# An attention decode block with gradients: the step order and weight layout of the Wo product, and the width of the V times do sums

## The chip, the cores and the metric

One core of one Trainium2 chip. The metric is the device time of one execution in microseconds (us). The core has a matrix engine (PE, with PEld for its weight loads), a vector engine (DVE), a scalar engine (ACT), GpSimd (POOL), and SP, which here only issues DMAs. Sixteen DMA engines move data between the chip's memory (DRAM) and the core's on-chip memory. PE writes its results to PSUM, in banks that each hold 512 float32 values on each of 128 partitions.

## The reference, cut to what matters

One token goes through a block of attention and MLP whose layer norms are modulated by a condition c. The kernel computes the output and the gradients of nine inputs.

```python
def _A_ref(x, k_cache, v_cache, wq, wo):          # 32 heads, 8192 keys, 192 wide
    q = (x @ wq).reshape(B, Sq, Hq, Dh).transpose(0, 2, 1, 3)
    scores = einsum('bhqd,bhkd->bhqk', q, k_cache) * Dh ** (-0.5)
    p = softmax(scores, axis=-1)
    o = einsum('bhqk,bhkd->bhqd', p, v_cache)
    return o.transpose(0, 2, 1, 3).reshape(B, Sq, Hq * Dh) @ wo

sa, ca, ga, sb, cb, gb = (silu(c) @ w_mod) in six parts of 640
h = layernorm(x) * (1 + ca) + sa
x = x + ga * _A_ref(h, ...)
h = layernorm(x) * (1 + cb) + sb
x = x + gb * _B_ref(h, ...)       # h + gelu(layernorm(h) @ w3) @ w4
_out, _vjp = jax.vjp(_f, x, k_cache, v_cache, wq, wo, w3, w4, c, w_mod)
return (_out, *_vjp(grad_out))
```

All arrays are bf16. x is 1 x 640, wq 640 x 6144, wo 6144 x 640, w_mod 640 x 3840, and each of k_cache and v_cache is 32 heads x 8192 x 192, 100 MB. The gradients of the two caches are as large again and are written out whole. (A first layer of `_B_ref` shifts the one token out of the sequence and adds zeros; it is left away here.)

## The kernel before, in words

**Tiles.** A head's K or V is 8192 rows of 192. It is moved in two halves of 1536 KB, each with 32 neighbouring rows on each of 128 partitions, so a partition receives 12288 neighbouring bytes. There are five such tiles for K (`big`), three for V in the forward (`fv`), and three more from the backward on (`bv`); K's tiles later hold the outputs dK and dV.

**Queues and order.** SP issues, in program order, every load of K, V and Wo in the forward, every load of V in the backward and every store of dK and dV. An issue that waits for its tile holds up those behind it. POOL issues Wo's loads for the backward and the stores of the gradients of Wo and w4. The order on PE, DVE and ACT is the order of the program: `pin_order` (L53) ties each instruction to the one before it on its engine, from the first forward product on.

**Forward, L592 to L659.** A loop over heads, with three heads in work at a time: in iteration i the scores of head i are made, and the scaled keys and values of head i-1 are summed. For the scores, `fwd_mult` multiplies a half of K by q on DVE (tile `prod`), `fwd_ssum` (L372) sums 192 columns down to 8 with 48 matmuls against an identity, `fwd_red` (L376) sums the last 8 on DVE; then come the maximum and the exponent. For head i-1, ACT (L407) and DVE (L414) scale K by the exponents, a quarter head at a time (tile `EK`), and PE multiplies V with the scaled K: `fwd_kvA` (L432), `fwd_kvB` (L443), and `fwd_kvK` (L449) for the sum of K. The result is a 192 x 192 matrix for a head, kept for the backward, and in one more column the unscaled output o.

Pairs of heads share 384 rows of Wo. `fwd_wo` (L460) loads them once per pair, 480 KB, as three blocks of 128 rows: row 128 c + p goes to partition p. `fwd_o` (L481, in odd iterations) divides o by the sum of the exponents and leaves it in three columns of `o_col_bf`, in that order of rows. In the next, even iteration `fwd_ao` (L520) multiplies the three blocks with the three columns in 15 matmuls of one column, into columns 408 to 412 of a PSUM tile `sm_ps`, and `fwd_ao_add` adds them to `ao_c` on DVE. Then `fwd_tot` (L476) sums the exponents of the two newer heads over the partitions, into columns 400 and 401 of the same `sm_ps`, and `fwd_rinv` (L479) inverts them on DVE. `sm_ps` has one buffer of one bank. The calls stand so in the loop:

```python
        if i % 2 == 0 and i >= 4:
            fwd_ao((i - 4) // 2, st[i - 3]["wo"], st[i - 1]["sm"])
            fwd_ao_add((i - 4) // 2, st[i - 1]["sm"])
        if p and i % 2 == 0:
            fwd_tot(i - 1, st[i - 1]["sm"])
```

On DVE a half's `fwd_mult` stands ahead of `fwd_ao_add`. The last two pairs have their Wo kept for the backward, which reads it in blocks of 128 rows.

**Middle, L660 to L889 and on.** The rest of the block: layer norms, the MLP and its gradient, down to the gradient of the attention output.

**Backward, L1249 to L1317.** A loop over heads from the last to the first. `bwd_mult` (L1017) multiplies a half of V in place by do, the gradient of that head's output, broadcast to all partitions (L132, tile `V_sb`); 24 matmuls a half (L1025), each with 256 columns (32 rows times 8), sum 192 products to 8 in the PSUM tile `dP_ps`. `bwd_ds` (L1051) sums the 8 on DVE, 512 numbers on each partition, and makes dS. `bwd_dk` (L1008, tile `dK`) makes the two halves of dK as dS times q on DVE and stores them. `bwd_dv` makes the next head's dV as probability times do, 20 of 32 rows on ACT (L1030) and 12 on DVE (L1008, tile `dV`), and stores it. V comes through a ring of six tiles. `hook` (the first ten heads, NPH = 10) makes do for the later pairs from Wo; in those ten heads other steps of the PSUM pool `psum_b` need banks too. Later jobs (J0 to J2) make the gradients of wq and w_mod, their sums at L1137 in the tile `js_ps`.

Of the kernel before, what the change touches and what calls it, by code (L numbers as in the profile page):

```python
# [9 lines left out]
BF16 = mybir.dt.bfloat16  # L10
# [10 lines left out]
def kernel(  # L21
# [26 lines left out]
    nc = tc.nc  # L48
# [16 lines left out]
    P = 128  # L65
# [5 lines left out]
    J = S // P  # L71
# [9 lines left out]
    DS = 8  # L81
# [15 lines left out]
    def bank_s(name):  # L97
        return bank("s", 2, name)
# [98 lines left out]
    def dve_copy(out, in_):  # L197
        nc.vector.tensor_copy(out=out, in_=in_)
# [120 lines left out]
    ao_c = ccol(NDC, "ao_c")  # L319
    fsm_cm = tc.tile_pool(name="fsmall", bufs=2, reuse_waits="tile")  # L320
    fsm = fsm_cm.__enter__()

    def head_split(h):
        if h % 2 == 0:
# [8 lines left out]
    def load_fwd(h, t, kind):  # L333
        if not 0 <= h < HQ:
            return
        if kind == "v":
            st[h]["V"].append(load_v(fv, h, t, (2 * h + t) % 3))
        elif (h, t) not in K_st:
            K_st[h, t] = load_k(h, t)
# [116 lines left out]
    def fwd_wo(h, st):  # L456
        if h % 2 == 1:
            c0 = 3 * (h // 2)
            st["wo"] = fwo.tile([P, 3, D], BF16, name="wo_t")
            nc.sync.dma_start(out=st["wo"], in_=wo_v[:, c0 : c0 + 3, :])  # L460

    def fwd_keep(h, st):
        (a0, a1), (b0, b1), bp, ca_, cb_ = head_split(h)
# [11 lines left out]
    def fwd_tot(h, sm):  # L475
        nc.tensor.matmul(sm[:, 400:402], lhsT=ones_mat_f, rhs=rowsum[:, h - 1 : h + 1], start=True, stop=True)  # L476
# [4 lines left out]
    def fwd_o(hp):  # L481
        c0 = 3 * hp
        for h in (2 * hp, 2 * hp + 1):
            _, _, bp, ca_, cb_ = head_split(h)
            mul(o_col_f[:, ca_ : ca_ + 1], MA_all[:, h, DH : DH + 1], rinv_bc[:, h : h + 1])
            mul(o_col_f[bp : bp + 64, cb_ : cb_ + 1], MB_all[bp : bp + 64, hp, DH : DH + 1], rinv_bc[bp : bp + 64, h : h + 1])
        dve_copy(o_col_bf[:, c0 : c0 + 3], o_col_f[:, c0 : c0 + 3])
# [20 lines left out]
    def fwd_o_last(h, st):  # L508
        _, _, bp, ca_, cb_ = head_split(h)
        c0 = 3 * (h // 2)  # L510
        sl = slice(bp, bp + 64)
        mul(o_col_f[:, ca_ : ca_ + 1], st["o_ps"][:, 0:1], rinv_bc[:, h : h + 1])
        mul(o_col_f[sl, cb_ : cb_ + 1], st["o_ps"][sl, 1:2], rinv_bc[sl, h : h + 1])
        dve_copy(o_col_bf[:, c0 : c0 + 3], o_col_f[:, c0 : c0 + 3])

    def fwd_ao(hp, wo, sm, c1=408):
        c0 = 3 * hp
# [74 lines left out]
    for i in range(1, HQ):  # L592
        c, p, pp = 2 <= i < HQ, 0 <= i - 1 < HQ, 0 <= i - 2 < HQ
        n = i + 1 < HQ
        if p:
            fwd_scale(i - 1, 0, st[i - 1])
        if pp:
            fwd_kvA(i - 2, 3, st[i - 2])
            fwd_kvB(i - 2, 3, st[i - 2])
            fwd_kvK(i - 2, 3, st[i - 2])  # L600
            fwd_keep(i - 2, st[i - 2])
            fwd_keepB(i - 2, st[i - 2])
            if i % 2 == 1:
                fwd_o((i - 2) // 2)
        load_fwd(i, 0, "v")
        if p:
            fwd_wo(i - 1, st[i - 1])
        if c:
            fwd_ssum(i, 0, st[i])
        if p:  # L610
            fwd_scale(i - 1, 1, st[i - 1])
            fwd_kv(i - 1, 0, st[i - 1])
        load_fwd(i + 1, 1, "k")
        if c:
            fwd_mult(i, 1, st[i])
        if i % 2 == 0 and i >= 4:
            fwd_ao((i - 4) // 2, st[i - 3]["wo"], st[i - 1]["sm"])
            fwd_ao_add((i - 4) // 2, st[i - 1]["sm"])
        if p and i % 2 == 0:
            fwd_tot(i - 1, st[i - 1]["sm"])  # L620
        if i % 2 == 1 and n:
            q_pb[(i + 1) // 2] = pair_bc(fsm, q_bf, (i + 1) // 2, "q_pb", st[max(i - 1, 1)]["sm"])
        if p:
            fwd_scale(i - 1, 2, st[i - 1])
            if i % 2 == 0:
                fwd_rinv(i - 1, st[i - 1]["sm"])
            fwd_kv(i - 1, 1, st[i - 1])
        load_fwd(i, 1, "v")
        if c:
            fwd_ssum(i, 1, st[i])  # L630
        if p:
            fwd_scale(i - 1, 3, st[i - 1])
            if i == 1:
                q_out(1, NWQ)
        if c:
            fwd_red(i, st[i])
        if p:
            fwd_kvA(i - 1, 2, st[i - 1])
        if c:
            fwd_comb(i, st[i])  # L640
        if p:
            fwd_kvK(i - 1, 2, st[i - 1])
        if c:
            fwd_max(i, st[i])
        if p:
            fwd_kvB(i - 1, 2, st[i - 1])
        if c:
            fwd_exp(i, st[i])
        load_fwd(i + 2, 0, "k")
        if i == HQ - 2:  # L650
            load_w(0)
        if i == HQ - 1:
            fwd_wo(i, st[i])
            load_w(1)
            load_w(2)
        if n:
            fwd_mult(i + 1, 0, st[i + 1])
        if n:
            fwd_pairs(i, st[i])  # L659
# [356 lines left out]

    def bwd_mult(h, t, parts=1):  # L1017
        if t == 0:
            bst[h]["dP_ps"] = bank_s("dP_ps").rearrange("p (j d) -> p j d", d=DS)
        n = JH // parts  # L1020
        for r in range(0, JH, n):
            V_sb = V_b[h][t][:, r : r + n, :]
            mul(V_sb, V_sb, vec_of(do_pb, h)[:, None, :].to_broadcast([P, n, DH]))
            for k in range(NDS):
                nc.tensor.matmul(bst[h]["dP_ps"][:, t * JH + r : t * JH + r + n, :], lhsT=ident_bf, rhs=V_sb[:, :, k * DS : (k + 1) * DS], start=(k == 0), stop=(k == NDS - 1))  # L1025
        freed.add(("v", h, t))

    def bwd_dv_act(o, h, t, lo=0, hi=NAV // 2):
# [206 lines left out]
    pairs_outer(o1[:, 26:JH, :], bst[HS[1]]["P2h"][:, 26:JH, :], vec_of(do_pb, HS[1]), JH - 26)  # L1235
    bwd_dv_store(o1, HS[1], 0, JQ, JH)
    psum_cm.__exit__(None, None, None)
    psum[0] = ctx.enter_context(tc.tile_pool(name="psum_b", bufs=1, space=bass.MemoryType.PSUM, reuse_waits="tile"))
    CB[0], SB[0] = 2, 512
    tw_cm.__exit__(None, None, None)  # L1240
    bso = ctx.enter_context(tc.tile_pool(name="bso", bufs=2, reuse_waits="tile"))
# [7 lines left out]
    for i in range(HQ):  # L1249
        h, nxt = HS[i], HS[i + 1] if i + 1 < HQ else None  # L1250
        if i % 2 == 1 and i > NPH and nxt is not None:
            bwd_dob(nxt // 2)
        for f in J0[i]:
            f()
        if i <= AHEAD:
            if i in SPLIT:
                bwd_pf(nxt)
            for t in range(2):
                bwd_mult(h, t, 2 if i == 0 else 1)
                if i == t == 0:  # L1260
                    ring_load()
                    c_first = fin_c(PS[0], 1)
                if i in SPLIT:
                    bwd_dv(nxt, t)
        if i not in EARLY:
            ring_load()
        if i - 1 in dq:
            fin_dq(*dq.pop(i - 1))
        if i == 0:
            fin_c_copy(PS[0], 1, c_first)  # L1270
        if nxt is not None and i not in SPLIT:
            if i > 0:
                bwd_pf(nxt)
            for t in range(0 if i > 0 else 1, 2):
                bwd_dv(nxt, t)
        if i in EARLY:
            ring_load()
        if i == 0:
            bwd_ds(h)
            dq_last(h)  # L1280
        if i < NPH:
            hook(i)
        if i == 3:
            bcast_cols(du_bf, 0, NFC, du_bc, act_copy)
        for f in J1[i]:
            f()
        if i > 0:
            bwd_ds(h)
        if i >= AHEAD and nxt is not None:
            for t in range(2):  # L1290
                bwd_mult(nxt, t)
        bwd_dk(h, 0)
        bwd_dk(h, 1)
        if i in cps:
            fin_c_copy(*cps.pop(i))
        if i == 1:
            mid_cols()
            job_mid()
            dve_copy(dmod_bf[:, 2 * NDC : 6 * NDC], dmod_c[:, 2 * NDC : 6 * NDC])
        if i == NPH - 1:  # L1300
            fin_dq(*dq.pop(i))
            mm_cm.__exit__(None, None, None)
            for nm, b in (("out", 2), ("bcp", 1)):
                side_cm.append(tc.tile_pool(name="side" + nm, bufs=b, side="right", reuse_waits="tile"))
                side[nm] = side_cm[-1].__enter__()
        for f in J2[i]:
            f()
        if i == I_SIDE:
            while side_cm:
                side_cm.pop().__exit__(None, None, None)  # L1310
            xt = ctx.enter_context(tc.tile_pool(name="xt", bufs=1, side="right", reuse_waits="tile"))
            for k in "xyz":
                tail_tiles[k] = (xt, "xt" + k)
            for n in range(len(ring) - NR, len(ring)):
                slot = ring_slot(n)
                tail_tiles[f"v{n - len(ring) + NR}"] = (bv if slot > 2 else fv, f"v{slot}")
            big_order[:] = tail_list(big_order[0:5] + ["x", "y", "z"])  # L1317
# [31 lines left out]
```

## Time and profile before

| what | value |
| --- | --- |
| time, median of 3 runs | 1374.94 us (1373.59 to 1375.22) |
| the profiled execution | 1375.21 us |
| its span, first to last instruction | 1373.4 us |
| mean granted TensorE clock in it | 0.785 |
| busy: PE, DVE, ACT, POOL | 881.4, 1062.8, 916.5, 21.5 us |
| moved by DMA | 569.26 MB in 65006 packets, 414 GB/s on average |
| forward | until about 534 us of the span |
| backward loop, with its last stores | from about 590 us to the end |

The profile is one execution. Engine rows give busy time and its share of the span, with instructions behind the x. In rows of groups, `out<-in` names the tiles that are written and read; behind the bar stand busy time, the mean of one instruction in ns, the idle time of the engine just before such instructions, and what ended most of it. Rows of a timeline start with the time of the first instruction and the length of the group, and have in brackets the idle time before it. The slices cut the span into 40 equal parts and show each engine's busy tenths. "DMA share" is the share of the 16 DMA engines' time in which a packet is under way.

### The profile page before, as it was taken

To read this page: it belongs to the slowest core of one execution; us is meant where nothing else is said; L and a number is where in the kernel's file an instruction comes from. 1 tells how busy PE (TensorE), PEld (TensorE's weight loads), DVE (VectorE), ACT (ScalarE), POOL (GpSimd) and SP (SyncE) were. 2 spreads that over 40 slices of the span, in tenths; PEclk is the share of its full clock that TensorE was granted. 3 is DMA by queue.
4 is the path that set the end of the run, shared out by engine and by line. 5 is a ranking of instruction groups with operands and counts; after the bars stand their busy time and mean duration, and the time that the engine had idled before them with its cause. 6 is when DMAs were issued, how large, how long until landed. Compare 5 with 4: busy or idle time off the path is not lost.

```text
span 1373.4 us, 28399 instructions
## 1 busy us (share of the span) xinstructions
PE 881.4 (64%) x11743; PEld 686.0 (50%) x11743; DVE 1062.8 (77%) x1196; ACT 916.5 (67%) x2564; POOL 21.5 (2%) x33
## 2 busy tenths in 40 slices
PE   3699999999999999757756664534334344224430
PEld 3577777777777777746645552322223223113330
DVE  3488878878878877899977877966768778669990
ACT  1388877877877876886766768645577564547960
POOL 0000000000000000000000000000000000000000
PEclk9799999999999999576676676666656757656665
DMA  9999999999999999899999999999999999999997
GB/s 392 412 413 420 420 419 419 419 412 414 418 409 421 419 407 387 336 394 424 423 419 426 424 424 427 422 428 425 428 425 424 427 427 428 426 428 427 428 429 309
DMA packets 65006, 569.26 MB, mean 414 GB/s; under 512 B 6444, under 2 KB 14124, under 8 KB 23404
## 3 DMA queue, kind: packets, MB, share of 16 engines
q1 hardware_dynamic: 61182, 550.73, 96.1%
q0 software_dynamic: 3664, 16.71, 3.0%
q8 instruction: 92, 1.51, 0.4%
q14 instruction: 38, 0.31, 0.1%
q10 hardware_dynamic: 30, 0.00, 0.0%
HBM read 341.51 MB, written 225.91 MB: 413 GB/s over the span
## 4 chain that ended last, share of the span: by engine, by line
DMA 38%; DVE 28%; PE 23%; ACT 4%; SPq 2%; issue 2%; DVEq 0%; ACTq 0%
DMA out_dram<-dV 25%; DVE prod L132 9%; PE ps_a L432 8%; DVE dK L1008 6%; DMA out_dram<-dK 6%; DVE V_sb L132 6%; PE S_ps L372 4%; DMA V_sb<-in_A_v_cache_dram 3%; PE dP_ps L1025 3%; PE ps_b L443 3%; PE kb_ps L449 2%; DVE dV L1008 2%; DMA K_sb<-in_A_k_cache_dram 2%; ACT dV L1030 2%; ACT EK L407 2%
## 5 line engine op out<-in xcount | busy, mean ns | idle before, releaser
L1030 ACT ACTIVATE dV<-do_pb,PF 128x192 bf16<-128x192 bf16 x1246 | 436.0, 440 | 173.3 <-DMA out_dram<-dV 132.2
L1025 PE MATMUL dP_ps<-V_sb,ident_bf 128*128 128x256 bf16 (+1 forms) x1584 | 237.0, 326 | 203.8 <-DVE V_sb L132 203.5
L407 ACT ACTIVATE EK<-K_sb,E_f 128x192 bf16<-128x192 bf16 x992 | 351.1, 442 | 4.0 <-PE kb_ps L302 2.6
L1025 PEld LDWEIGHTS <-ident_bf 128*128 128x128 bf16 x1584 | 182.2, 119 | 260.9 <-DVE V_sb L132 170.7
L1008 DVE TENSOR_TENSOR dK<-dS,q_pb 128x6144 bf16<-128x6144 bf16 x64 | 212.6, 3354 | 15.7 <-DMA out_dram<-dK 12.0
L132 DVE TENSOR_TENSOR prod<-K_sb,q_pb 128x6144 bf16<-128x6144 bf16 x64 | 214.3, 3349 | 3.0 <-DMA K_sb<-in_A_k_cache_dram 3.0
L132 DVE TENSOR_TENSOR V_sb<-V_sb,do_pb 128x6144 bf16<-128x6144 bf16 (+1 forms) x66 | 212.3, 3253 | 0.0
L432 PE MATMUL ps_a<-EK,V_sb 128*128 128x193 bf16 x1984 | 195.7, 252 | 3.2 <-DMA V_sb<-in_A_v_cache_dram 3.2
L432 PEld LDWEIGHTS <-V_sb 128*128 128x128 bf16 x1984 | 168.3, 100 | 21.1 <-issue 12.5
L1008 DVE TENSOR_TENSOR dV<-P2h,do_pb 128x2304 bf16<-128x2304 bf16 (+2 forms) x67 | 89.8, 1353 | 113.9 <-DMA out_dram<-dV 111.8
L414 DVE TENSOR_TENSOR EK<-K_sb,P2h 128x1536 bf16<-128x1536 bf16 x124 | 117.4, 948 | 0.0
L443 PE MATMUL ps_b<-EK,V_sb 128*64 128x193 bf16 x1984 | 109.0, 252 | 0.0
L372 PE MATMUL S_ps<-prod,ident_bf 64*64 64x256 bf16 x3072 | 98.8, 275 | 11.4 <-DVE prod L132 11.4
L372 PEld LDWEIGHTS <-ident_bf 64*64 64x64 bf16 x3072 | 84.3, 108 | 31.0 <-issue 26.9
L1137 PE MATMUL js_ps<-V_sb,ident_bf 128*128 128x512 bf16 (+1 forms) x100 | 40.7, 587 | 88.8 <-DVE V_sb L132 88.8
L443 PEld LDWEIGHTS <-V_sb 128*64 128x64 bf16 x1984 | 81.8, 110 | 19.7 <-issue 16.1
L393 ACT ACTIVATE E_f<-sm_ps,negm 128x64 f32<-128x64 f32 x31 | 9.7, 314 | 102.4 <-DVE negm L391 102.4
L376 DVE TENSOR_REDUCE S<-S_ps 128x128 f32<-128x1024 f32 x32 | 39.2, 1225 | 47.9 <-PE S_ps L372 47.9
L1137 PEld LDWEIGHTS <-ident_bf 128*128 128x128 bf16 x100 | 13.5, 135 | 111.2 <-issue 110.5
L449 PE MATMUL kb_ps<-EK,hot_bf 128*32 128x384 bf16 x992 | 64.0, 335 | 0.0
L195 ACT CAST do_pb<-bc_ps 128x384 bf16<-128x384 f32 x15 | 7.1, 470 | 51.1 <-PE bc_ps L191 51.1
L1075 ACT ACTIVATE dwo<-dao_bc,o_col_f 128x640 bf16<-128x640 bf16 x48 | 36.1, 817 | 0.0
(256 smaller groups left out, 707.8 us busy)
## 6 DMA issues: line engine op xcount, KB each, us to landing
V_sb<-in_A_v_cache_dram SPq DMA_DIRECT2D x125, 1536.0 KB, 14.2
K_sb<-in_A_k_cache_dram SPq DMA_DIRECT2D x64, 1536.0 KB, 14.7
out_dram<-dK SPq DMA_DIRECT2D x64, 1536.0 KB, 23.6
out_dram<-dV SPq DMA_DIRECT2D x61, 1536.0 KB, 26.0
wq<-in_A_wq_dram SPq DMA_DIRECT2D x3, 2560.0 KB, 33.9
wo_t<-in_A_wo_dram SPq DMA_DIRECT2D x16, 480.0 KB, 14.7
out_dram<-dwo POOLq DMA_DIRECT2D x16, 480.0 KB, 9.7
V_sb<-in_A_wq_dram SPq DMA_DIRECT2D x5, 1536.0 KB, 20.7
```

What stands on the lines that cost most here:

```text
L132: nc.vector.tensor_tensor(out=out, in0=a, in1=b, op=ALU.mult)
L372: nc.tensor.matmul(st["S_ps"][c0 : c0 + 64, r, t * JH : (t + 1) * JH, :], lhsT=ident_bf[64 * r : 64 * r + 64, 64 * r : 64 * r + 64], rhs=p ...
L376: nc.vector.reduce_sum(out=st["S2"], in_=st["S_ps"], axis=AX.X)
L407: nc.scalar.activation(out=st["EK"][q][:, jj, 0:DH], in_=K_st[h, t][:, r * JQ + jj, :], func=ACT.Copy, scale=st["E_f"][:, j : j + 1])
L414: nc.vector.tensor_tensor(out=EK[:, NA:JQ, 0:DH].rearrange("p j (d r) -> p j d r", r=2), in0=K_st[h, t][:, r * JQ + NA : (r + 1) * JQ, :]. ...
L432: nc.tensor.matmul(st["A_ps"][:, 0:n], lhsT=V_sb[:, r * JQ + jj, a0:a1], rhs=EK[:, jj, 0:n], start=(q == 0 and jj == 0), stop=(q == 3 and ...
L443: nc.tensor.matmul(st["B_ps"][g : g + 64, 0:n], lhsT=V_sb[:, r * JQ + jj, b0:b1], rhs=EK[:, jj, 0:n], start=(q == 0 and jj < 2), stop=(q = ...
L449: nc.tensor.matmul(kb_ps[g : g + 32, 0 : 2 * DH], lhsT=hot_bf[:, HQ - 1 - h : 2 * HQ - 1 - h], rhs=EK[:, jj : jj + 2, 0:DH], start=(h == 0 ...
L1008: nc.vector.tensor_tensor(out=o.rearrange("p j (d r) -> p j d r", r=2), in0=pairs[:, :, None, :].to_broadcast([P, n, NP2, 2]), in1=vec.rea ...
L1025: nc.tensor.matmul(bst[h]["dP_ps"][:, t * JH + r : t * JH + r + n, :], lhsT=ident_bf, rhs=V_sb[:, :, k * DS : (k + 1) * DS], start=(k == 0 ...
L1030: nc.scalar.activation(out=o[:, jj, :], in_=vec_of(do_pb, h), func=ACT.Copy, scale=bst[h]["PF"][:, t * JH + jj : t * JH + jj + 1])
L1137: nc.tensor.matmul(ps, lhsT=ident_bf, rhs=w[:, k * m : (k + 1) * m], start=(k == 0), stop=(k == n // m - 1))
```

## The change

There are three edits.

1. In even iterations `fwd_tot` is called ahead of `fwd_ao` and `fwd_ao_add`. Its columns of `sm_ps` are others than theirs.
2. For the first 14 pairs Wo is loaded with three neighbouring rows on each partition: row 3 p + c of the pair goes to partition p, block c, 3840 neighbouring bytes for a partition. `o_col_bf` has to follow: a new `fwd_o_rows`, called in the even iteration after the pair's `fwd_o`, picks the rows with nine matmuls of one column against a shifted identity (`sel_bf`, read with a step of three) into columns 403 to 405 of `sm_ps`, and one copy on DVE puts them back into `o_col_bf`. Building `sel_bf` takes two DVE instructions before the forward loop. The last two pairs stay as they were.
3. After the tenth head of the backward the PSUM pool `psum_b` is left, and a new pool takes its place with 1024 columns, two banks, for each `dP_ps`. `bwd_mult` then sums to 16 columns, not 8: 12 matmuls a half, each with 512 columns (32 rows times 16). The reduction at L1051 reads 1024 numbers on each partition. The first ten heads stay as they were, and so does everything that POOL and SP issue, in kind and order, but for the layout of Wo.

```diff
@@ -319,6 +319,9 @@
     ao_c = ccol(NDC, "ao_c")
     fsm_cm = tc.tile_pool(name="fsmall", bufs=2, reuse_waits="tile")
     fsm = fsm_cm.__enter__()
+    sel_bf = fsm.tile([P, 5 * P], BF16, name="sel_bf", bufs=1)
+    nc.vector.memset(sel_bf, 0.0)
+    nc.vector.tensor_copy(out=sel_bf[:, 2 * P : 3 * P], in_=ident_bf)
 
     def head_split(h):
         if h % 2 == 0:
@@ -457,7 +460,8 @@
         if h % 2 == 1:
             c0 = 3 * (h // 2)
             st["wo"] = fwo.tile([P, 3, D], BF16, name="wo_t")
-            nc.sync.dma_start(out=st["wo"], in_=wo_v[:, c0 : c0 + 3, :])
+            src = A_wo[c0 * P : (c0 + 3) * P, :].rearrange("(p c) r -> p c r", c=3) if h // 2 < HH - 2 else wo_v[:, c0 : c0 + 3, :]
+            nc.sync.dma_start(out=st["wo"], in_=src)
 
     def fwd_keep(h, st):
         (a0, a1), (b0, b1), bp, ca_, cb_ = head_split(h)
@@ -512,6 +516,14 @@
         mul(o_col_f[:, ca_ : ca_ + 1], st["o_ps"][:, 0:1], rinv_bc[:, h : h + 1])
         mul(o_col_f[sl, cb_ : cb_ + 1], st["o_ps"][sl, 1:2], rinv_bc[sl, h : h + 1])
         dve_copy(o_col_bf[:, c0 : c0 + 3], o_col_f[:, c0 : c0 + 3])
+
+    def fwd_o_rows(hp, sm):
+        c0 = 3 * hp
+        for c in range(3):
+            for k in range(3):
+                lo = (2 - k) * P + c
+                nc.tensor.matmul(sm[:, 403 + c : 404 + c], lhsT=sel_bf[:, lo : lo + 3 * P - 2 : 3], rhs=o_col_bf[:, c0 + k : c0 + k + 1], start=(k == 0), stop=(k == 2))
+        dve_copy(o_col_bf[:, c0 : c0 + 3], sm[:, 403:406])
 
     def fwd_ao(hp, wo, sm, c1=408):
         c0 = 3 * hp
@@ -602,6 +614,8 @@
             fwd_keepB(i - 2, st[i - 2])
             if i % 2 == 1:
                 fwd_o((i - 2) // 2)
+            elif 0 <= (i - 4) // 2 < HH - 2:
+                fwd_o_rows((i - 4) // 2, st[i - 1]["sm"])
         load_fwd(i, 0, "v")
         if p:
             fwd_wo(i - 1, st[i - 1])
@@ -613,11 +627,11 @@
         load_fwd(i + 1, 1, "k")
         if c:
             fwd_mult(i, 1, st[i])
+        if p and i % 2 == 0:
+            fwd_tot(i - 1, st[i - 1]["sm"])
         if i % 2 == 0 and i >= 4:
             fwd_ao((i - 4) // 2, st[i - 3]["wo"], st[i - 1]["sm"])
             fwd_ao_add((i - 4) // 2, st[i - 1]["sm"])
-        if p and i % 2 == 0:
-            fwd_tot(i - 1, st[i - 1]["sm"])
         if i % 2 == 1 and n:
             q_pb[(i + 1) // 2] = pair_bc(fsm, q_bf, (i + 1) // 2, "q_pb", st[max(i - 1, 1)]["sm"])
         if p:
@@ -1016,13 +1030,15 @@
 
     def bwd_mult(h, t, parts=1):
         if t == 0:
-            bst[h]["dP_ps"] = bank_s("dP_ps").rearrange("p (j d) -> p j d", d=DS)
+            w = SB[0] // J
+            bst[h]["dP_ps"] = bank("s", 2, "dP_ps", SB[0]).rearrange("p (j d) -> p j d", d=w)
+        w = SB[0] // J
         n = JH // parts
         for r in range(0, JH, n):
             V_sb = V_b[h][t][:, r : r + n, :]
             mul(V_sb, V_sb, vec_of(do_pb, h)[:, None, :].to_broadcast([P, n, DH]))
-            for k in range(NDS):
-                nc.tensor.matmul(bst[h]["dP_ps"][:, t * JH + r : t * JH + r + n, :], lhsT=ident_bf, rhs=V_sb[:, :, k * DS : (k + 1) * DS], start=(k == 0), stop=(k == NDS - 1))
+            for k in range(DH // w):
+                nc.tensor.matmul(bst[h]["dP_ps"][:, t * JH + r : t * JH + r + n, :], lhsT=ident_bf, rhs=V_sb[:, :, k * w : (k + 1) * w], start=(k == 0), stop=(k == DH // w - 1))
         freed.add(("v", h, t))
 
     def bwd_dv_act(o, h, t, lo=0, hi=NAV // 2):
@@ -1235,7 +1251,8 @@
     pairs_outer(o1[:, 26:JH, :], bst[HS[1]]["P2h"][:, 26:JH, :], vec_of(do_pb, HS[1]), JH - 26)
     bwd_dv_store(o1, HS[1], 0, JQ, JH)
     psum_cm.__exit__(None, None, None)
-    psum[0] = ctx.enter_context(tc.tile_pool(name="psum_b", bufs=1, space=bass.MemoryType.PSUM, reuse_waits="tile"))
+    psum_cm = tc.tile_pool(name="psum_b", bufs=1, space=bass.MemoryType.PSUM, reuse_waits="tile")
+    psum[0] = psum_cm.__enter__()
     CB[0], SB[0] = 2, 512
     tw_cm.__exit__(None, None, None)
     bso = ctx.enter_context(tc.tile_pool(name="bso", bufs=2, reuse_waits="tile"))
@@ -1300,6 +1317,9 @@
         if i == NPH - 1:
             fin_dq(*dq.pop(i))
             mm_cm.__exit__(None, None, None)
+            psum_cm.__exit__(None, None, None)
+            psum[0] = ctx.enter_context(tc.tile_pool(name="psum_s", bufs=1, space=bass.MemoryType.PSUM, reuse_waits="tile"))
+            SB[0] = 1024
             for nm, b in (("out", 2), ("bcp", 1)):
                 side_cm.append(tc.tile_pool(name="side" + nm, bufs=b, side="right", reuse_waits="tile"))
                 side[nm] = side_cm[-1].__enter__()
```

## Prediction

> **What bounds the kernel now.** I began with the page: busy shares and the forty slices.
>
> ```profile
> PE 881.4 (64%) x11743; PEld 686.0 (50%) x11743; DVE 1062.8 (77%) x1196; ACT 916.5 (67%) x2564; POOL 21.5 (2%) x33
> PE   3699999999999999757756664534334344224430
> DVE  3488878878878877899977877966768778669990
> DMA  9999999999999999899999999999999999999997
> GB/s 392 412 413 420 420 419 419 419 412 414 418 409 421 419 407 387 336 394 424 423 419 426 424 424 427 422 428 425 428 425 424 427 427 428 426 428 427 428 429 309
> ```
>
> A slice is 34.3 us. The forward fills the first sixteen, the backward the rest. The DMA row is full in nearly all of them, and PE is nearly full in the forward as well. Stretches of 50 us say it more finely (columns: length, then busy time and instructions of PE, PEld, DVE, ACT and POOL, the granted clock, the DMA share, GB/s):
>
> ```profile
> 150.00:200.00 50.00, 48.46 (x855) 38.29 (x853) 41.82 (x62) 40.05 (x119) 0.00 (x0) 0.97 1.01 420
> 300.00:350.00 50.00, 48.45 (x893) 38.30 (x891) 40.67 (x62) 37.48 (x110) 0.00 (x0) 1.00 1.00 410
> 530.00:540.00 10.00, 10.00 (x185) 7.70 (x174) 8.82 (x16) 8.16 (x24) 0.00 (x0) 1.00 0.92 348
> 850.00:900.00 50.00, 22.05 (x124) 13.99 (x123) 39.85 (x21) 28.38 (x75) 1.52 (x2) 0.70 1.01 423
> 1250.00:1300.00 50.00, 23.75 (x156) 17.98 (x156) 49.72 (x28) 41.64 (x121) 0.00 (x0) 0.72 1.01 428
> 1330.00:1374.00 44.00, 0.17 (x2) 0.00 (x0) 10.69 (x5) 0.00 (x0) 0.00 (x0) 0.54 0.78 331
> ```
>
> A share of 1.01 is a full DMA (packets of one engine overlap a little). So the backward moves as many bytes as it can, and PE and DVE have room in it until about 1250. In the forward two things are full together, PE (48.5 of 50) and DMA. To tell which one leads I looked at who waits, and at how long a K load takes to land, early (first of these lines) and late (second) in the forward:
>
> ```profile
> DMA to landing us min/median/max: 8.0/12.3/13.1
> DMA to landing us min/median/max: 15.3/15.5/17.4
> L132 DVE TENSOR_TENSOR prod<-K_sb,q_pb 128x6144 bf16<-128x6144 bf16 x64 | 214.3, 3349 | 3.0 <-DMA K_sb<-in_A_k_cache_dram 3.0
> PE sm_ps L476 <- DVE ao_c L135: 15.1, 13, 1.9
> ```
>
> The landing time grows by 3 us over the forward, so loads are issued slightly faster than they land: compute is the quicker of the two and is eating its lead. Its waits for K sum to 3.0 us only, because the lead has just been used up. PE, for its part, loses 15.1 us in 13 waits to the order of two steps. My reading: the forward is bound by the DMA, with compute less than 1 us behind in a pair of heads of 31 us. The backward is bound by the DMA outright.
>
> **The change, part by part.**
>
> *Sum of the exponents ahead of the Wo product.* PE in one even iteration:
>
> ```profile
> 226.82 1.50 PE L372 MATMUL S_ps<-prod,ident_bf 64*64 64x256 bf16 x48 [0.16 <-DVE prod L132]
> 230.96 0.53 PE L520 MATMUL sm_ps<-o_col_bf,wo_t 128*128 128x1 bf16 x15
> 232.55 0.38 PE L476 MATMUL sm_ps<-rowsum,ones_mat_f 128*128 128x2 f32 x2 [1.07 <-DVE ao_c L135]
> 232.79 1.52 PE L432 MATMUL ps_a<-EK,V_sb 128*128 128x193 bf16 x16
> 214.15 0.17 DVE L198 CAST o_col_bf<-o_col_f 128x3 bf16<-128x3 f32 x1
> ```
>
> The sum (L476) waits until DVE has added the Wo product to ao_c, and that addition stands behind a 3.3 us product on DVE. With the sum first, PE goes from Wo's 15 matmuls straight to ps_a: 1.07 us less in this iteration, 15.1 us in all. What is late next is the scaled K of that quarter, and ACT and DVE had finished it before PE began to wait. No DMA issue moves.
>
> *What the new row order costs.* Each of 14 pairs gets nine matmuls of one column: at Wo's rate of 0.53/15 they take 0.32 us, at three times that (their weights are read with a step of three) 0.95 us. They stand ahead of S_ps, which waits 0.16 us for DVE anyway. I take 0.32, since the 15 matmuls of Wo are the same shape. DVE gets one copy of 0.17 us, which waits for those nine matmuls; behind it on DVE stands the scaling of the next quarter, which PE needs about 3 us later. PE thus gains 1.07 - 0.32, about 0.7 us a pair. But this shortens the side that is ahead already: **PE's gain of some 10 us buys nothing by itself**, it turns into waits for K and V. The two instructions that build the selection matrix fall into the first 30 us, where DVE is mostly idle.
>
> *Three neighbouring rows of Wo per partition.* 480 KB go as 128 packets of 3840 B, not 384 of 1280 B, on 16 DMA engines: 8 for 24 on each. The prices come from three short stretches: a K load (22 to 24 us, 12288 B packets), Wq (45 to 47, 4096 B) and mostly Wo (329.3 to 330.2).
>
> ```profile
> DMA packets 70, 0.85 MB, mean 424 GB/s; under 512 B 1, under 2 KB 1, under 8 KB 1
> q1 hardware_dynamic: 70, 0.85, 100.1%
> ...
> DMA packets 201, 0.82 MB, mean 412 GB/s; under 512 B 0, under 2 KB 0, under 8 KB 201
> q1 hardware_dynamic: 201, 0.82, 102.8%
> ...
> DMA packets 154, 0.37 MB, mean 411 GB/s; under 512 B 6, under 2 KB 138, under 8 KB 138
> q1 hardware_dynamic: 153, 0.35, 101.0%
> ```
>
> First: 1.001 x 32 engine-us / 69 = 464 ns for 12288 B. Second: 1.028 x 32 / 201 = 164 ns for 4096 B. Third: 1.010 x 14.4 = 14.5 us, less 15 large packets (7.0) and six tiny ones, leaves 7.5 us for 132, so 57 ns for 1280 B. A 3840 B packet lies between 145 ns (in proportion to 12288 B) and 154 (to 4096 B). An engine then spends 24 x 57 = 1.37 us on one Wo load before and 8 x 153 = 1.22 after: 0.15 us less, at most 0.21. Over 14 loads that is **2.1 us** (0 to 2.9), and it is the DMA's own time, which the forward pays. I take the 4096 B price, the nearest size.
>
> The Trainium skill, "DMA: Bandwidth & Descriptors", section Specifications, puts the smallest transfer for full line rate at 512 B; by that both sizes run alike and this term is 0. The rows above disagree: 22 B/ns at 1280 B against 26 B/ns at 12288 B. By that rule the sum would keep its other term only.
>
> *The end of the forward.* The last K load was issued at 516.1, landed 14.7 us later at 530.8, and its product began at 532.25 behind other work on DVE:
>
> ```profile
> L236 SPq DMA_DIRECT2D K_sb<-in_A_k_cache_dram x1: 328/328/328, 516.1 to 516.1; - x1
> DMA to landing us min/median/max: 14.7/14.7/14.7
> 532.25 3.35 DVE L132 TENSOR_TENSOR prod<-K_sb,q_pb 128x6144 bf16<-128x6144 bf16 x1
> ```
>
> Compute was 1.4 us late there, and the DMA (0.92 in 530 to 540) ran short because its next loads waited for compute. A quicker compute meets the landing at once: **1.4 us** (0 to 3, the upper end being the rate lost in that row, (420 - 348)/420 of 10 us, with as much again behind it).
>
> *Backward sums by 512 columns.* From the eleventh head on, 22 heads take 24 matmuls of 512 columns for 48 of 256, and DVE's reduction reads 1024 columns, not 512:
>
> ```profile
> L1051 DVE TENSOR_REDUCE dP<-dP_ps 128x64 f32<-128x512 f32 x6 | 4.1, 684 | 0.0
> L376 DVE TENSOR_REDUCE S<-S_ps 128x128 f32<-128x1024 f32 x32 | 39.2, 1225 | 47.9 <-PE S_ps L372 47.9
> L1025 PE MATMUL dP_ps<-V_sb,ident_bf 128*128 128x256 bf16 (+1 forms) x1584 | 237.0, 326 | 203.8 <-DVE V_sb L132 203.5
> L1137 PE MATMUL js_ps<-V_sb,ident_bf 128*128 128x512 bf16 (+1 forms) x100 | 40.7, 587 | 88.8 <-DVE V_sb L132 88.8
> L1008 DVE TENSOR_TENSOR dV<-P2h,do_pb 128x2304 bf16<-128x2304 bf16 (+2 forms) x67 | 89.8, 1353 | 113.9 <-DMA out_dram<-dV 111.8
> ```
>
> DVE pays 1225 - 684 = 541 ns a head, 11.9 us in all. PE gains 48 x 326 - 24 x 587 = 1.6 us a head, and PE mostly waits for DVE there (203.5 us). Until about 1250 DVE itself waits 111.8 us for stores to free its tiles, so the 541 ns go into that wait. After 1250 DVE is full, and five heads make it 2.7 us late. It ends its work near 1337 with 0.331 x 44 = 14.6 MB still to move; the stores behind it then have 2.7 us less lead, out of more than 30. So this part costs nothing and gains nothing. If that cover were gone it would cost its 11.9 us. The exchanged PSUM pool only adds waits on a reduction and a copy that DVE has finished before the product PE waits for.
>
> *Sum.* 2.1 + 1.4 = 3.5 us. The profiled execution took 1375.2 us (its span 1373.4 and 1.8 around it), 0.3 over the median of the three runs, 1374.94. From the median: **1371.4 us**, 0.25% less.
>
> **The rivals.**
>
> *The DMA gets its lost rate back as well.* Between 300 and 350 it moved 410 GB/s where 150 to 200 had 420: 1.2 us lost in one stretch. The page's slices 9 to 15 (412, 414, 418, 409, 421, 419, 407) lie 5.7 GB/s under 420 on average, 240 us x 5.7/420 = 3.3 us. If that loss came from compute's hold-ups (loads issued late), a quicker PE returns it: 3.5 + 3.3 = 6.8 us, 1368.1. For it: the loss appears only once the lead is used up. Against it: with compute waiting for K, hold-ups go on.
>
> *No change to speak of.* Packets cost by their bytes alone, or an engine that lags sets each landing and is not the one relieved; then only the end of the forward gives something, 1.4 us: 1373.5.
>
> *Slower: DVE's longer reductions come through.* If stores reach the DMA later by 541 ns in each of the 22 heads, because DVE's waits for tiles shrink by less than its work grows, the backward grows by up to 11.9 us: 1371.4 + 11.9 = 1383.3. It decides from the point where the DMA share between 850 and 1250 falls below 1.0. For it: DVE stands in the chain (the full row after 1250). Against: its 40 of 50 busy at 850 to 900, with the DMA at 1.01.
>
> *The change doesn't do what it says.* If the sum still waited on DVE (for the copy of the new rows), PE would keep its 15 us and gain only losses. The forward would then follow PE: 14 x 0.32 - 2.1, about 2.4 us slower, 1377.3. The copy stands ahead of the long product, so I give this little.
>
> **How the numbers follow.** Forecast 0.42 (its own range 1370 to 1373, by the bounds of its two terms), lost rate returned 0.27, no change 0.22, slower by DVE 0.06, the wait that stays 0.03. A measurement here tells 0.2%, 2.75 us, from no change. Faster by more: 0.27 and about three quarters of the forecast's 0.42, 0.59. Slower by more: 0.08, DVE's whole chance and part of the last. The rest, 0.33, is within. The range goes from 1367.5 (the returned rate with the upper price of Wo) to 1376.0 (no change and a little of DVE's or PE's cost); what it leaves out is DVE's cost in full and a gain beyond 7.4 us.
>
> **What would show it.** No idle time before L476's matmuls, and the 15.1 us turned into waits of prod or ps_a for DMA loads. 14 x 384 = 5376 fewer packets under 2 KB (3584 fewer in all), and some 420 GB/s or more between 300 and 500. A reduction of 1225 ns in 22 heads with the DMA share still 1.01 to the end. Backward starts some 3 to 4 us earlier, and its length is unchanged. It is wrong if the backward's length changes, or if PE stays busy without waiting for loads while the forward gets shorter by more than 7 us.

## The result, and the profile after

The changed kernel takes **1371.43 us** (median of 10 executions, 1370.0 to 1372.58); the kernel before took 1375.04 beside it (10 executions, 1373.59 to 1375.3). The ratio is 0.9976, with a 95% interval of 0.9968 to 0.9984: 3.3 us less, 2.2 to 4.4. The forecast was 1371.4. The profiled execution took 1371.65 us, its span is 1369.9. The sum came out as forecast; the experiments show that two of its terms did not.

The page of the changed kernel, with its two kinds of reduction and its sums from the view of groups (lines are numbered anew: L372 is now L375, L476 is L480, L1025 is L1041, L1051 is L1067):

```profile
PE 872.3 (64%) x11341; PEld 621.7 (45%) x11341; DVE 1078.5 (79%) x1212; ACT 916.5 (67%) x2564; POOL 21.5 (2%) x33
DMA packets 61420, 569.21 MB, mean 416 GB/s; under 512 B 6445, under 2 KB 8749, under 8 KB 19821
```

```profile
L132 DVE TENSOR_TENSOR prod<-K_sb,q_pb 128x6144 bf16<-128x6144 bf16 x64 | 214.6, 3354 | 37.3 <-DMA K_sb<-in_A_k_cache_dram 36.9 <-ACT E_f L396 0.5
L480 PE MATMUL sm_ps<-rowsum,ones_mat_f 128*128 128x2 f32 x32 | 6.1, 262 | 0.0
L1041 PE MATMUL dP_ps<-V_sb,ident_bf 128*128 128x512 bf16 x528 | 157.1, 468 | 179.6 <-DVE V_sb L132 179.6
L1067 DVE TENSOR_REDUCE dP<-dP_ps 128x64 f32<-128x1024 f32 x22 | 26.8, 1218 | 0.2 <-PE dP_ps L1041 0.2
```

PE no longer waits at the sum of the exponents (0.0, where 15.1 us stood), and DVE's product waits 36.9 us for loads of K, where it was 3.0: compute runs into the DMA, as forecast. Under 2 KB there are 14124 - 8749 = 5375 fewer packets (forecast 5376). The reduction of 1024 columns takes 1218 ns. The timeline of PE around one sum shows that it costs nothing any more, and a new wait near the end of the forward, for the last half of V:

```profile
512.29 0.38 PE L480 MATMUL sm_ps<-rowsum,ones_mat_f 128*128 128x2 f32 x2
512.53 0.51 PE L532 MATMUL sm_ps<-o_col_bf,wo_t 128*128 128x1 bf16 x15
...
543.35 0.95 PE L497 MATMUL sm_ps<-E_all,V_sb 128*128 128x1 bf16 x32 [1.35 <-DMA V_sb<-in_A_v_cache_dram]
```

Before, the same matmuls came later and did not wait for V:

```profile
545.49 0.94 PE L493 MATMUL sm_ps<-E_all,V_sb 128*128 128x1 bf16 x32 [0.26 <-DVE rinv_bc L479]
```

The same stretches as shown of before (busy time and instructions of PE, PEld, DVE, ACT and POOL, clock, DMA share, GB/s):

```profile
300.00:350.00 50.00, 46.95 (x856) 37.34 (x852) 41.89 (x63) 39.66 (x118) 0.00 (x0) 1.00 1.01 421
...
530.00:540.00 10.00, 8.60 (x153) 6.77 (x153) 7.58 (x12) 4.18 (x14) 0.00 (x0) 1.00 0.92 349
...
850.00:900.00 50.00, 20.33 (x72) 7.98 (x71) 41.41 (x22) 28.75 (x78) 1.53 (x2) 0.74 1.01 424
...
1250.00:1300.00 50.00, 22.20 (x84) 8.99 (x84) 49.72 (x27) 39.14 (x113) 0.00 (x0) 0.70 1.01 428
```

Between 300 and 350 the DMA moves 421 GB/s, not 410. At 530 to 540 it runs as short as before in this profile (0.92, 349 against 348), although compute there is quicker. The backward is full of transfers, as it was.

**Where the 3.5 us of the two profiles lie.** I added up the bytes of all packets in the order of their ends and read off when each kernel had moved the same amount. The changed kernel is 1.2 us ahead at 120 MB (290 us), 2.6 at 144 MB (348 us), 3.6 at 216 MB (522 us), 3.2 at 240 MB (589 us) and 2.9 at 552 MB (1324 us): nothing is won in 735 us of backward, and 0.3 us is lost. Then 0.6 us more come in the drain of the last stores. One profile scatters by about 1 us in such figures, as the kernel before against itself shows below, so the parts had to be run by themselves.

### The profile page after: what moved, and what is told of

The parts are those of the page before. It is cut to its first block, busy times and chain, and to the rows that moved or that the text cites. A ratio compares the mean times of both kernels' runs of the same rounds, so it can differ in the third digit from the quotient of the medians.

```text
span 1369.9 us, 27612 instructions
## 1 busy us (share of the span) xinstructions
PE 872.3 (64%) x11341; PEld 621.7 (45%) x11341; DVE 1078.5 (79%) x1212; ACT 916.5 (67%) x2564; POOL 21.5 (2%) x33
## 2 busy tenths in 40 slices
DMA packets 61420, 569.21 MB, mean 416 GB/s; under 512 B 6445, under 2 KB 8749, under 8 KB 19821
## 4 chain that ended last, share of the span: by engine, by line
DMA 47%; DVE 27%; PE 13%; ACT 7%; SPq 2%; issue 2%; DVEq 0%; ACTq 0%
DMA out_dram<-dV 17%; DMA V_sb<-in_A_v_cache_dram 16%; DMA K_sb<-in_A_k_cache_dram 13%; DVE V_sb L132 8%; DVE dK L1022 7%; ACT EK L410 5%; DVE prod L132 4%; PE ps_a L435 3%; PE dP_ps L1041 3%; DVE dV L1022 3%; PE ps_b L446 2%; PE S_ps L375 2%; SPq L236 1%; PE kb_ps L452 1%; DMA out_dram<-dK 1%
## 5 line engine op out<-in xcount | busy, mean ns | idle before, releaser
L1041 PE MATMUL dP_ps<-V_sb,ident_bf 128*128 128x512 bf16 (+2 forms) x1056 | 232.2, 393 | 216.5 <-DVE V_sb L132 216.4
L1041 PEld LDWEIGHTS <-ident_bf 128*128 128x128 bf16 x1056 | 119.0, 118 | 327.5 <-DVE V_sb L132 181.7
L132 DVE TENSOR_TENSOR prod<-K_sb,q_pb 128x6144 bf16<-128x6144 bf16 x64 | 214.6, 3354 | 37.3 <-DMA K_sb<-in_A_k_cache_dram 36.9
L435 PE MATMUL ps_a<-EK,V_sb 128*128 128x193 bf16 x1984 | 191.6, 248 | 3.1 <-DMA V_sb<-in_A_v_cache_dram 3.1
L435 PEld LDWEIGHTS <-V_sb 128*128 128x128 bf16 x1984 | 163.9, 98 | 20.5 <-issue 12.3
L375 PE MATMUL S_ps<-prod,ident_bf 64*64 64x256 bf16 x3072 | 98.8, 275 | 23.6 <-DVE prod L132 23.6
L375 PEld LDWEIGHTS <-ident_bf 64*64 64x64 bf16 x3072 | 84.6, 108 | 38.8 <-issue 36.6
L1153 PE MATMUL js_ps<-V_sb,ident_bf 128*128 128x512 bf16 (+1 forms) x100 | 37.1, 545 | 86.3 <-DVE V_sb L132 86.3
L1153 PEld LDWEIGHTS <-ident_bf 128*128 128x128 bf16 x100 | 12.9, 129 | 108.9 <-issue 106.0
```

The lines of the kernel that those rows point to most:

```text
L132: nc.vector.tensor_tensor(out=out, in0=a, in1=b, op=ALU.mult)
L375: nc.tensor.matmul(st["S_ps"][c0 : c0 + 64, r, t * JH : (t + 1) * JH, :], lhsT=ident_bf[64 * r : 64 * r + 64, 64 * r : 64 * r + 64], rhs=p ...
L435: nc.tensor.matmul(st["A_ps"][:, 0:n], lhsT=V_sb[:, r * JQ + jj, a0:a1], rhs=EK[:, jj, 0:n], start=(q == 0 and jj == 0), stop=(q == 3 and ...
L1153: nc.tensor.matmul(ps, lhsT=ident_bf, rhs=w[:, k * m : (k + 1) * m], start=(k == 0), stop=(k == n // m - 1))
```

## The experiments

Each was timed beside the kernel before on its chip; ratios are to that, with 95% intervals. All twelve stand here.

**One part alone.** First edit alone (`fwd_tot` called ahead of `fwd_ao`):

```diff
+        if p and i % 2 == 0:
+            fwd_tot(i - 1, st[i - 1]["sm"])
         if i % 2 == 0 and i >= 4:
             fwd_ao((i - 4) // 2, st[i - 3]["wo"], st[i - 1]["sm"])
             fwd_ao_add((i - 4) // 2, st[i - 1]["sm"])
-        if p and i % 2 == 0:
-            fwd_tot(i - 1, st[i - 1]["sm"])
```

> The kernel before with the sum of the exponents moved ahead of the Wo product, and nothing else. Theory (the DMA sets the pace; PE's 15 us of waits matter only through the four spells of half clock that follow them, after each of which the DMA slows): the spells after 100 us go, the dips at 300 to 310, 400 to 410 and 490 to 500 go with them, and the kernel takes 1.5 to 2.5 us less, about 1373.0. Waits of DVE's product for K grow from 3 us to 20 or more. Rival (PE and DMA share the bound, PE's order is the whole gain): 1371.5. Second rival (the clock spells have nothing to do with the order): they stay, and under 0.5 us is gained.

Measured: 1374.53 us, ratio 0.9999 (0.9990 to 1.0008). The waits for K grew as expected. Of the four spells of half clock (stretches of 3.41 us in which the granted clock is 0.5) one is left after 100 us. The gain did not come, so neither the waits nor the spells set the time. Its groups and two stretches:

```profile
L132 DVE TENSOR_TENSOR prod<-K_sb,q_pb 128x6144 bf16<-128x6144 bf16 x64 | 214.5, 3352 | 37.9 <-DMA K_sb<-in_A_k_cache_dram 37.9
L476 PE MATMUL sm_ps<-rowsum,ones_mat_f 128*128 128x2 f32 x32 | 6.1, 262 | 0.0
```

```profile
300.00:350.00 50.00, 46.28 (x837) 36.87 (x837) 41.32 (x61) 39.28 (x117) 0.00 (x0) 1.00 1.01 420
...
530.00:540.00 10.00, 8.63 (x149) 6.79 (x148) 8.38 (x12) 4.68 (x16) 0.00 (x0) 1.00 0.91 337
```

PE's 15 us are gone and the rate is back at 420, yet the time is that of before. Second edit alone (rows of Wo, `fwd_o_rows`, `sel_bf`), and third edit alone (`bwd_mult`, the pool `psum_s`), each as in the diff above:

> The kernel before with Wo by three neighbouring rows and the nine matmuls and the copy that go with it; the sum of the exponents stays behind the Wo product. Theory: fewer packets give about 0.13 us a pair, 1.8 us; PE has 0.4 us more work in a pair and keeps its 1.1 us wait, which leaves it slower than the DMA now, so about half of it comes through: 1374 (1373 to 1376), half-clock spells still there. Rival (the packets cost by their bytes, so nothing is gained, and PE's 14 x 0.4 us come through): 1378 to 1381.

Measured: 1373.53 us, 0.9994 (0.9985 to 1.0003), not clear of no change by itself. PE's extra work does not come through.

> The kernel before with the backward sums of 512 columns alone. Theory: 1375.0, within 0.5 us of before, the reductions' 11.9 us hidden in DVE's waits for its tiles. Rival (the changed kernel's last stores end 0.6 us closer to the middle of the backward than before, so the wide sums gain): 1374.4 or less. Second rival (the reductions come through): up to 1387.

Measured: 1374.06 us, 0.9992 (0.9983 to 1.0001), on the side of the first rival but not clear of no change.

**Two parts together.** Without the third edit, without the second, without the first, and the whole change again:

> The changed kernel without the backward sums of 512 columns. Theory: as fast as the changed kernel, 1371.4 within 0.5. Rival (the wide sums gain in the tail): 1372 or more. Second rival (the wide sums cost): 1370.5 or less, and then it would be the better version.

Measured: 1372.54 us, 0.9984 (0.9975 to 0.9993): 1 us over the theory, as its first rival has it.

> The changed kernel with Wo in its old layout (sum first and wide sums). From the single parts so far: sum first alone -0.2 us, wide sums alone -0.6. Theory (sum first buys nothing, wide sums nothing, what the single runs show beside that is scatter): 1374.7 within 0.7. Rival (the wide sums give about 1 us in the tail, where the last stores drain): 1373.7 or less.

Measured: 1373.14 us, 0.9992 (0.9983 to 1.0001). The ratio gives 0.9992 x 1374.8 = 1373.7, so this is the rival's case.

> The changed kernel with the sum of the exponents behind the Wo product again. Theory (only the packets of Wo count, sum first is worth nothing): near 1372.8, at most 0.7 above the kernel with sum and rows. Rival (with the new rows PE needs its 15 us back, so sum first is what lets the rows pay): 1373.7 or more. If the wide sums give 1 us by themselves: 1371.8.

Measured: 1372.12 us, 0.9977 (0.9969 to 0.9986): the rows pay without the sum first, and the wide sums add to them.

> The changed kernel once more, beside the two above on one chip: 1371.4 within 0.7. If the wide sums are worth nothing, it comes out level with the earlier run of sum and rows (0.9984 of before); if they give about 1 us, at 0.9976.

Measured: 1371.41 us, 0.9975 (0.9965 to 0.9985).

> The kernel before against itself: a ratio of 1.000, and a second profile of it, which shows how far cumulative bytes, the spells of half clock and the end of the forward scatter between executions of the same kernel. Theory: the spells come at other times, and the lead at 520 us scatters by some 1 us.

Measured: 1374.57 us, 0.9999 (0.9990 to 1.0008). Its profile has three spells of half clock between 100 and 530 us, at other times than the first profile's four, and is 0.8 us ahead of it at 216 MB.

With the kernel before as 1, these are all eight combinations. The worth of a part is the mean of its four differences; eight ratios, each within 0.0009, make each mean uncertain by 0.0009 x sqrt(8) / 4, some 0.9 us.

| part | four differences of ratio, in 0.0001 | mean, us |
| --- | --- | --- |
| rows of Wo | -6 (alone), -15 (with sum), -15 (with wide), -16 or -17 (with both) | -1.8 |
| wide sums | -8 (alone), -7 (with sum), -17 (with rows), -8 or -9 (with both) | -1.4 |
| sum first | -1 (alone), -10 (with rows), 0 (with wide), -1 or -2 (with both) | -0.4 |

The three add up to the 3.6 us between the medians. The rows and the wide sums are clear of zero; the sum first is not.

**What the rows cost and save.**

```diff
-            nc.sync.dma_start(out=st["wo"], in_=wo_v[:, c0 : c0 + 3, :])
+            for lo, hi in ((0, D // 2), (D // 2, D)) if h // 2 < HH - 2 else ((0, D),):
+                nc.sync.dma_start(out=st["wo"][:, :, lo:hi], in_=wo_v[:, c0 : c0 + 3, lo:hi])
```

> The sum of the exponents first, as in the run of that alone, with Wo in its old layout but each load of the first 14 pairs split into two of half a row, 640 B for each packet in place of 1280: 768 packets a pair, not 384. Theory (a packet costs a fixed part beside its bytes: 57 ns at 1280 B and 153 at 3840 give 37.5 ns per 1000 B and 9 ns fixed): 48 x 33 - 24 x 57 = 0.2 us a pair on each DMA engine, 3 us slower than the sum first alone, about 1376. Rival (packets cost by their bytes): the same as the sum first alone, within 0.5 us.

Measured: 1377.19 us, 1.0018 (1.0010 to 1.0027), 0.0019 or 2.6 us over the sum first alone. Twice the packets cost, as the theory has it (with 14 more issues beside them). The second kernel of this kind has the extra work without the layout:

```diff
+                lo = 2 * P if k == c else 0
+                nc.tensor.matmul(sm[:, 403 + c : 404 + c], lhsT=sel_bf[:, lo : lo + P], rhs=o_col_bf[:, c0 + k : c0 + k + 1], start=(k == 0), stop=(k == 2))
+        dve_copy(o_col_bf[:, c0 : c0 + 3], sm[:, 403:406])
```

> The sum of the exponents first, and nine matmuls and one copy in each of 14 pairs as the new layout has them, but against the identity in place and two blocks of zeros, so that the columns come back unchanged, with Wo loaded in its old layout. Theory (PE is ahead of the DMA once the sum stands first, by about 0.7 us a pair): the nine matmuls cost nothing, the same as the sum first alone, within 0.5 us. Rival (PE still sets the pace): 14 x 0.4 = 5.6 us slower than that.

Measured: 1374.77 us, 1.0001 (0.9992 to 1.0010): nothing, as expected. Packets of the forward, from the traces (mean of all between 60 and 520 us): 35.3 ns for 640 B, 57.8 for 1280 B, 152.2 for 3840 B, 470 for 12288 B.

**What DVE's longer reductions cost.**

```diff
-        nc.vector.reduce_sum(out=dP, in_=bst[h]["dP_ps"], axis=AX.X)
+        for _ in range(1 if HQ - 1 - h < NPH else 2):
+            nc.vector.reduce_sum(out=dP, in_=bst[h]["dP_ps"], axis=AX.X)
```

> The changed kernel with the reduction of 1024 columns done twice in each of the 22 later heads, the second over the first: 22 x 1.22 = 26.8 us more on DVE in the backward. Theory (DVE waits about 100 us for stores, the DMA is the bound until the last heads): up to 1250 us all is hidden, behind it DVE is full and five heads come 6 us later, and the stores behind them have over 30 us of lead: under 1.5 us slower, 1371.4 to 1373. Rival (DVE's work comes through in each head): up to 26.8 us slower, 1398.

Measured: 1371.76 us, 0.9977 (0.9968 to 0.9986), level with the changed kernel. Two stretches of it, one in the full backward and one at its end:

```profile
850.00:900.00 50.00, 21.55 (x74) 8.41 (x72) 43.48 (x25) 28.61 (x77) 1.52 (x2) 0.70 1.01 422
...
1340.00:1350.00 10.00, 0.00 (x0) 0.00 (x0) 9.90 (x6) 0.00 (x0) 0.00 (x0) 0.71 1.01 431
```

DVE is busier (43.5 of 50, not 41.4) and works until 1350, and its last store is issued at 1350.9, 9.4 us after the changed kernel's. The DMA stays full all the same, with what was queued before.

**Where the wide sums gain.** That left 1.4 us which nothing in my account explained. The profiles put them at the very end. Nothing but stores is left there, and the view of stretches shows how the 16 DMA engines run dry; first the kernel before, then the changed one:

```profile
1355.00:1360.00 5.00, 0.00 (x0) 0.00 (x0) 0.00 (x0) 0.00 (x0) 0.00 (x0) 0.50 1.01 430
1360.00:1365.00 5.00, 0.00 (x0) 0.00 (x0) 0.00 (x0) 0.00 (x0) 0.00 (x0) 0.50 0.60 256
1365.00:1369.00 4.00, 0.00 (x0) 0.00 (x0) 0.00 (x0) 0.00 (x0) 0.00 (x0) 0.50 0.17 71
1369.00:1373.00 4.00, 0.00 (x0) 0.00 (x0) 0.00 (x0) 0.00 (x0) 0.00 (x0) 0.50 0.04 18
```

```profile
1355.00:1360.00 5.00, 0.00 (x0) 0.00 (x0) 0.00 (x0) 0.00 (x0) 0.00 (x0) 0.50 0.88 374
1360.00:1365.00 5.00, 0.00 (x0) 0.00 (x0) 0.00 (x0) 0.00 (x0) 0.00 (x0) 0.50 0.26 111
1365.00:1369.00 4.00, 0.00 (x0) 0.00 (x0) 0.00 (x0) 0.00 (x0) 0.00 (x0) 0.50 0.05 22
```

One engine of 16 is a share of 0.06. Before, the engines end between 1360.5 and 1367.0, and one works alone until 1371.9. After, all but one have ended by 1364.0, and the last ends at 1368.3. What else could load single engines was the queue of kind "instruction": packets of 16 KB that each take one engine for about 1 us. After 590 us there are 18 with sum and rows (first line) and 13 with the whole change (second):

```profile
q8 instruction: 18, 0.29, 0.1%
```

```profile
q8 instruction: 13, 0.21, 0.1%
```

In the 22 heads the wide sums save 22 x 2 x 12 matmuls and as many weight loads, 1056 instructions of PE; at five packets for them that is some 210 to a packet, near the 256 that the Trainium skill, "Runtime: NRT & Kernel Launch", section "Instruction fetch mechanics", gives for a block of 16 KiB. To test it I raised the instructions and left everything else:

```diff
-            for k in range(DH // w):
-                nc.tensor.matmul(bst[h]["dP_ps"][:, t * JH + r : t * JH + r + n, :], lhsT=ident_bf, rhs=V_sb[:, :, k * w : (k + 1) * w], start=(k == 0), stop=(k == DH // w - 1))
+            m = 8 if w > DS else n
+            for q in range(0, n, m):
+                lo = t * JH + r + q
+                for k in range(DH // w):
+                    nc.tensor.matmul(bst[h]["dP_ps"][:, lo : lo + m, :], lhsT=ident_bf, rhs=V_sb[:, q : q + m, k * w : (k + 1) * w], start=(k == 0), stop=(k == DH // w - 1))
```

> The changed kernel with each half's 12 backward sums of 512 columns cut into 48 of 128 columns for the 22 later heads: the same bytes, the same reduction of 1024 columns, the same columns through PE, but 3168 instructions more for PE (counting its weight loads), which have to be fetched by the DMA: some 12 more fetches of 16 KB at about 1 us each, after 590 us. Theory (the 1.5 us that the wide sums give in the drain of the last stores come from five fewer fetches, which weigh on the DMA engine that ends last): the last engine falls back behind the second by 5 us or more, not 2 to 4, and the kernel takes 2 to 4 us more than the changed kernel, 1373.5 to 1375.5. Rival (the gain comes from the wide reduction, the exchanged PSUM pool or what DVE does): as the changed kernel, 1371.4 within 0.7. Second rival (the extra PE work itself comes through): the stretch from 600 to 1320 us gets longer by over 1 us.

Measured: 1374.94 us, 1.0007 (0.9997 to 1.0016), 3.5 us over the changed kernel by the medians and 4.3 by the ratios, where the theory has 2 to 4; the last engine ends 5.8 us behind the second. Its sums, its fetches after 590 us and its last stretches:

```profile
L1044 PE MATMUL dP_ps<-V_sb,ident_bf 128*128 128x128 bf16 x2208 | 168.2, 253 | 181.9 <-DVE V_sb L132 181.8
```

```profile
q8 instruction: 25, 0.41, 0.2%
```

```profile
1365.00:1369.00 4.00, 0.00 (x0) 0.00 (x0) 0.00 (x0) 0.00 (x0) 0.00 (x0) 0.50 0.06 28
1369.00:1373.00 4.00, 0.00 (x0) 0.00 (x0) 0.00 (x0) 0.00 (x0) 0.00 (x0) 0.50 0.01 6
```

Twelve fetches more, and one engine works alone through all of 1365 to 1369 and beyond. By the bytes of all profiles:

| backward sums | profiles | fetches of 16 KB after 590 us | last engine behind the second, us | 565 MB to the last byte, us |
| --- | --- | --- | --- | --- |
| 256 columns | 7 | 17 or 18 | 3.4 to 5.5, mean 4.5 | 17.2 to 18.1, mean 17.7 |
| 512 columns | 6 | 13 or 14 | 1.9 to 4.3, mean 3.1 | 15.7 to 17.3, mean 16.4 |
| 48 of 128 columns | 1 | 25 | 5.8 | 19.4 |

From 240 MB to 552 MB all fourteen profiles lie between 734.3 and 735.6 us, so it is the end that differs: 1.3 us for five fetches and 3.0 for twelve (one profile), about a quarter of a microsecond each. The fetched bytes are counted in this; at 425 GB/s they make 0.2 and 0.5 us of it. PE's own time is not the cause: that stretch of 735 us is no longer with the short sums, and last stores that are issued late cost nothing in the run with two reductions.

The trace does not name the engine of a packet, but its packets can be linked: 3 or 4 ns before one ends the next one of its engine starts (some 14 ns before a fetch ends). After 1150 us this gives sixteen chains of packets in each profile, with some 15 of 8900 links that do not fit. The fourteen profiles have 47 fetches there. Within a profile no two of them are on the same engine, and 3 of the 47 are on the engine that ends last, which is an even share of one in sixteen. That engine is late already: at 1150 us it has 4.6 to 8.7 us more of data to move than the average engine. So the fetches do not pile up on the engine that ends last. At an even share a fetch of 1 us costs each engine 0.06 us, a quarter of what was measured. That the number of PE's instructions sets the length of the end is shown by the dose; how it does so, beyond the fetched packets themselves, stays open.

**Where the sum first loses its gain.** By the same count of bytes, as means of the profiles of each kind:

| Wo, sum | profiles | 216 MB moved at | from there to 240 MB | 240 MB moved at | last K load lands |
| --- | --- | --- | --- | --- | --- |
| old rows, sum behind | 3 | 521.2 | 67.1 | 588.3 | 530.2 |
| old rows, sum first | 3 | 519.7 | 68.9 | 588.7 | 529.9 |
| new rows, sum behind | 2 | 519.1 | 67.4 | 586.5 | 527.9 |
| new rows, sum first | 5 | 518.1 | 68.6 | 586.7 | 528.4 |
| half rows, sum first | 1 | 523.5 | 69.8 | 593.3 | 533.3 |

The sum first puts the DMA 1.0 to 1.5 us ahead by 216 MB, and gives it back, 1.2 to 1.8 us, before 240 MB. The last K load lands at the same time with it and without. From that landing to the first backward sum on PE it takes 46.4 to 48.1 us in all fourteen. On the way PE waits longer for the last half of V (the wait shown at 543.35 above): 1.3 to 2.3 us in the nine profiles with the sum first, none in three of the five with the sum behind and 0.7 and 1.0 in the other two. Why the last K load lands no earlier, with the DMA ahead at 216 MB, stays open.

## Why the prediction was right, and where it was not

- **What bounds the kernel: right.** Taking 15 us of waits from PE alone left the time as it was (0.9999), and adding 14 x 9 matmuls did too (1.0001).
- **Packets of Wo, 2.1 us: right in mechanism and nearly in size.** Measured 1.8, with an uncertainty of 0.9. The packets themselves cost 24 x 57.8 = 1.39 us before and 8 x 152.2 = 1.22 after, 0.17 a pair and 2.4 in all. At 640 B it is 48 x 35.3 = 1.69, 0.31 a pair more, 4.3 in all; the sum first with half rows was 3.8 us late at 216 MB and 2.6 late in time. So the rule of the Trainium skill, "DMA: Bandwidth & Descriptors", section Specifications, that line rate is reached from 512 B on, does not hold here: 640 B ran at 18 B/ns, 12288 B at 26.
- **"A quicker compute meets the landing at once: 1.4 us": this step failed.** Compute does meet it: the last product starts 0.4 to 1.9 us after the landing in the five profiles with the sum behind, and at most 0.1 after it in the nine with the sum first. But then the next thing is late: the last half of V lands 1.35 us after PE is ready for it, in the row at 543.35 above. And the DMA is as idle at 530 to 540 as before with the sum first and old rows (0.91 to 0.93 in three profiles, 0.90 to 0.92 with the sum behind); the changed forward scatters there, 0.92 to 1.01 in four profiles. The first edit measured 0.4, within 0.9 of nothing.
- **"This part costs nothing and gains nothing": the first half right, the second wrong.** The longer reductions are hidden, even doubled. But the wide sums take away PE instructions, which are fetched through the same 16 DMA engines, and the end gets 1.3 us shorter with five fetches fewer (1.4 in time). The sum of the prediction put this part at nothing and had no term for instructions at all. Two readings in it are off without bearing on the sum: DVE ended its work before at 1340.8 us, not near 1337, and the matmuls of 512 columns took 468 ns, not 587.
- So the total was met by luck: a term that was 1 us too high and one that was 1.4 us too low cancel. "Backward starts 3 to 4 us earlier, and its length is unchanged" was half right: by the means it started 1.6 us earlier (588.3 to 586.7 at 240 MB), its body kept its length, and its drain got shorter. A changed length was one of the prediction's own signs of being wrong, and the drain is it.
- **Rivals.** Lost rate returned: it does come back (421 for 410, where 410 is the lowest of its kind: between 300 and 350 the five profiles with the sum behind have 410 to 420, the nine with it first 418 to 423), and is given back at the end of the forward, so it is worth nothing. No change: refuted by the half rows. Slower by DVE: refuted by the double reduction. The wait that stays: 0.0 us at L480. No version here beats the changed kernel; without the sum first it is level with it (0.9977).

## What to carry to other kernels

When the DMA is full, count everything that it moves, the instructions too: 528 matmuls fewer were worth 1.4 us here, although PE was idle for more than half of the backward. A stage's gain counts only if the landing that starts the next stage comes earlier; add up bytes against time in both traces to see where a lead is won and where it is given back. A sum that comes out right does not show that its terms are: run the parts, in all combinations if they are few.

## What the runs showed of the hardware

- An instruction fetch of 16 KB takes about 1 us on a DMA engine, and there were 92 on that queue before. The Trainium skill, "Runtime: NRT & Kernel Launch", section "Instruction fetch mechanics", calls the cost of crossing a 16 KiB boundary mostly hidden. Here nothing of it shows in 735 us of the backward, but the end of the kernel was about 0.25 us longer for each fetch more after 590 us.
- Spells of half clock, 3.41 us each, came between 100 and 530 us one to four times in each of the five profiles with the sum behind. With the sum first there were none in six profiles, one in two and two in one. Each of the 17 spells starts 1.5 to 3.1 us after the beginning of a single wait of PE, 1.1 to 2.2 us long, with at most 0.16 us of other idle time in one piece in the 6.9 us ahead of it. So one such wait seems to be enough, but most bring none on (13 at the sum before, four spells), and the spells come at times that differ from one execution to the next (169, 295, 391 and 487 us in one, 107, 359 and 455 in another).
